# A Strassen pair of third tiles across two halves, in a fused local-attention and ReGLU kernel

## The chip, the cores and the metric

The kernel runs on one core of one Trainium2 chip. The metric is the device time of one execution in microseconds (us). Before the change it is 241.64 us, the median of 3 runs (241.13 to 242.92). Times with two decimals below are from one profiled execution, counted from the start of its span.

## The reference

Attention over 4 batches, 8 heads, 768 positions and head size 64, in which every row sees 8 global keys and a window of 96 local ones, with a bias by distance. Its output, 3072 tokens of 512, goes through a gated feed-forward layer with 1536 hidden columns:

```python
scores = scale * np.matmul(q, k.transpose(0, 1, 3, 2))
keep = is_global | is_local
scores = np.where(keep, scores + bias, -1e9)
a = np.exp(scores - max); a = a / sum(a)
attn_out = np.matmul(a, v)
x = attn_out.transpose(0, 2, 1, 3).reshape(B * S, H * D)
gate = np.maximum(x @ w_gate, 0.0)
val = x @ w_val
return gate * val @ w_out
```

## The kernel before

The work is cut into eight *halves*, numbered c or s from 0 to 7: half a batch each, 384 query positions, three tiles of 128 tokens. For each half there are three kinds of work.

- **Early pieces** (L377): casts of q and k on GpSimd, transposes by DMA, copies that put the keys in order.
- **Attention pieces** (L493), for four pairs of heads p. `QK(p)` is three pieces: `pair_scores` (L386), eight or ten score matmuls into four banks of the `x` PSUM pool (5 banks), with the exps of group 0 on ScalarE (`pair_exps`, L403); then the exps of group 1 and the mask products of group 0 on VectorE (`masks`, L349); then the masks of group 1. `AV(p)` is two pieces, one for each head of the pair (L416): four or five matmuls, a log on ScalarE, and after the second the exp that gives the reciprocal. `N(p)` (L443) is two VectorE products that write the normalized result into `xT`, the input of the feed-forward part.
- **Feed-forward pieces** (`ffn_pieces`, L509). First the weights stage, twelve columns fc of `gate` (four matmuls of 128x384, then a Relu on ScalarE) and `val` (four matmuls, then a VectorE product that writes `ht[:, fc]`). They use the `ff` PSUM pool (3 banks) in turn. Then the output stage: the third tile of the half is multiplied with `w_out` directly (`outp`, twelve matmuls of 128x512), and the first and second tiles together by Strassen's scheme.

The Strassen scheme takes the two tiles as the two rows of a block matrix, the hidden dimension split in two as its columns, and `w_out` as a 2 by 2 block matrix. Seven block products p1 to p7 of six 128x256 matmuls each take the place of eight. Sums and differences of `w_out` blocks (`late["bs"]`) are made once. Sums and differences of `ht` blocks (`cb`, `ad`, `de`) are made for each half on VectorE, some behind the vals of the weights stage (`behind`, L632) and the rest in the output stage (L654). p4, p3 and p1 are copied from PSUM by ScalarE; p2, p5, p6 and p7 are added by VectorE; p6 accumulates into p3's bank and p7 into p1's, and so these banks come free only after the adds of p6 and p7. Results lie in `osb` (3 buffers) and are stored by SyncE's queue, at the very end one of them by ScalarE's.

The order is written by hand: each engine runs its instructions in the order in which the program issues them. `weave` (L664) issues the feed-forward pieces of half c one after the other, counting up their weights (0.65 each, less for the begin), and puts in other pieces by their place, a fraction of the total: the attention of half c+1, spread from 0.0 to 0.8 of half c (for c = 2 from 0.07 to 0.82), and the early pieces of half c+2, from 0.25 to 0.75. So in half 7 no attention is beside the feed-forward work. The first items of a half are `begin` (L546; gate 0 and val 0 on the first three quarters of `xT`) and then the last quarter of gate 0 and of val 0.

In half 6 the issue order around its start and its end is this (other pieces in brackets):

```text
begin [QK0 group 0] g0 [QK0 group 1] v0 g1 [QK0 masks] v1 [QK1 group 0] g2 [QK1 group 1] ...
... g11 [AV2.1] v11 [QK3 masks] o.0 [N2] o.1 [AV3.0] ad o.2 [AV3.1] cb o.3 [N3] p4 de p3 p1 p2 p5 p6 p7
```

Of the kernel before, what the change touches and what calls it, by code (L numbers as in the profile page):

```python
# [8 lines left out]
FP32 = mybir.dt.float32  # L9
BF16 = mybir.dt.bfloat16  # L10
AF = mybir.ActivationFunctionType
ALU = mybir.AluOpType
# [3 lines left out]
def kernel(  # L16
# [12 lines left out]
    nc = tc.nc  # L29
# [4 lines left out]
    DM = H * D  # L34
    DFF = moe_w_gate.shape[1]
    N_DC = DM // 128
    N_FC = DFF // 128
    HP = H // 2
    QH = S // 2
    NN = 3  # L40
# [3 lines left out]
    NHALF = 2 * B  # L44
# [8 lines left out]
    for half in range(2):  # L53
        for j in range(NT):
            w0 = PK * j - 128 * half
            a, b_ = max(0, w0), min(128, w0 + WQ)
# [15 lines left out]
    late = {}  # L72

    PSUM = bass.MemoryType.PSUM
    psum = {}
# [20 lines left out]
    wo_sb = const.tile([128, N_FC, DM], BF16)  # L96
# [264 lines left out]
    def piece_cast(s, p, i):  # L361
        of = (ks_of, qs_of)[i]
        nc.gpsimd.tensor_copy(  # L363
            kqc[:, :, i].rearrange("t n (h d) -> t h n d", d=D)[:, 2 * p : 2 * p + 2],
            of[s][:, 2 * p : 2 * p + 2, :].rearrange("t e (n d) -> t e n d", n=NN))

    def piece_x(s, n):
        nc.sync.dma_start_transpose(
            out=kqT[s % 2].rearrange("d i p t -> d (i p) t")[:, :, n * 128 : (n + 1) * 128],
            in_=kqc[:, n].rearrange("t i z -> t (i z)"))  # L370
# [6 lines left out]
    def early_pieces(s):  # L377
        out = [(0.0, lambda p=p, i=i: piece_cast(s, p, i)) for i in range(2) for p in range(HP)]
        out += [(0.0, lambda n=n: piece_x(s, n)) for n in range(NN)]
        out += [(0.0, lambda p=p: piece_order(s, p)) for p in range(HP)]  # L380
        return out
# [111 lines left out]
    def attention_pieces(s):  # L493
        QK = lambda p: [(0.15, lambda g=g: piece_qk(s, p, g)) for g in range(3)]
        AV = lambda p: [(0.29, lambda e=e: piece_av(s, p, e)) for e in range(2)]
        N = lambda p: [(0.0, lambda: piece_norm(s, p))]
        g = QK(3)
        a = AV(2)
        gap = [(0.0, lambda: None)]
        return (QK(0) + QK(1) + AV(0) + N(0) + gap + QK(2) + AV(1) + N(1) + gap  # L500
                + g[0:1] + a[0:1] + g[1:2] + a[1:2] + g[2:3] + N(2) + AV(3) + N(3))
# [3 lines left out]
    out_v = out.rearrange("(s p n) d -> s n p d", p=128, n=NN)  # L505

    begin_of = {}

    def ffn_pieces(c):  # L509
        ht = ht_pool.tile([128, N_FC, QH], BF16, name="ht")  # L510
        st = {}
# [38 lines left out]
            if c == 2:  # L550
                product(wg, "g", 1, 0, N_DC - 1)


        N2, D2 = N_FC // 2, DM // 2
        tiles_ = [slice(n * 128, (n + 1) * 128) for n in range(2)]

        def sums_of(name, *shape):
            if name not in st:
                st[name] = late["sums"].tile([128, *shape], BF16, name=name)
            return st[name]  # L560

        cb = lambda: sums_of("cb", N2, 2, 128)
        ad = lambda: sums_of("ad", N2, 128)
        de = lambda: sums_of("de", N_FC, 128)

        def sum_cb(i0, i1):
            nc.vector.tensor_tensor(cb()[:, i0:i1].rearrange("f i n t -> f i (n t)"), ht[:, i0:i1, 0:256],
                                    ht[:, N2 + i0 : N2 + i1, 0:256], op=ALU.add)

        def sum_ad(i0, i1):  # L570
            nc.vector.tensor_tensor(ad()[:, i0:i1], ht[:, i0:i1, tiles_[0]],
                                    ht[:, N2 + i0 : N2 + i1, tiles_[1]], op=ALU.add)

        def sum_de(i0, i1):
            x, y = (1, 0) if i0 < N2 else (0, 1)
            nc.vector.tensor_tensor(de()[:, i0:i1], ht[:, i0:i1, tiles_[x]], ht[:, i0:i1, tiles_[y]],
                                    op=ALU.subtract)

        def block(key, pool, left, right, start, stop):
            if start:  # L580
                st[key] = psum[pool].tile([128, 512], FP32, name=f"{pool}_ps")
            for i in range(N2):
                nc.tensor.matmul(st[key][:, 0:D2], lhsT=left(i), rhs=right(i),  # L583
                                 start=start and i == 0, stop=stop and i == N2 - 1,
                                 skip_group_check=not start)
            return st[key][:, 0:D2]

        c0, c1 = slice(0, D2), slice(D2, DM)
        bs = lambda name: lambda i: late["bs"][name][:, i]
        V2 = nc.vector.tensor_tensor  # L590

        def store(n, cols, eng=nc.sync):
            eng.dma_start(out=out_v[c, n][:, cols], in_=st["r", n][:, cols])

        def p4():
            for n in range(2):
                st["r", n] = late["osb"].tile([128, DM], FP32, name="osb")
            ps = block("d", "ff", lambda i: ht[:, N2 + i, tiles_[1]], bs("b21-b11"), True, True)
            nc.scalar.copy(st["r", 0][:, c0], ps)

        def p3():
            ps = block("c", "ff", lambda i: ht[:, i, tiles_[0]], bs("b12-b22"), True, True)
            nc.scalar.copy(st["r", 0][:, c1], ps)

        def p1():
            ps = block("a", "ff", lambda i: ad()[:, i], bs("b11+b22"), True, True)
            nc.scalar.copy(st["r", 1][:, c1], ps)

        def p2():
            ps = block("b", "x", lambda i: cb()[:, i, 1], lambda i: wo_sb[:, i, c0], True, True)  # L610
            V2(st["r", 1][:, c0], ps, st["r", 0][:, c0], op=ALU.add)
            V2(st["r", 1][:, c1], st["r", 1][:, c1], ps, op=ALU.subtract)

        def p5():
            ps = block("e", "x", lambda i: cb()[:, i, 0], lambda i: wo_sb[:, N2 + i, c1], True, True)
            V2(st["r", 0][:, c1], ps, st["r", 0][:, c1], op=ALU.add)
            V2(st["r", 0][:, c0], st["r", 0][:, c0], ps, op=ALU.subtract)
            if c == NHALF - 1:
                store(1, c0)
                store(0, c1)  # L620

        def p6():
            ps = block("c", "ff", lambda i: de()[:, i], bs("b11+b12"), False, True)
            V2(st["r", 1][:, c1], ps, st["r", 1][:, c1], op=ALU.add)
            store(1, slice(0, DM) if c < NHALF - 1 else c1, nc.sync if c < NHALF - 1 else nc.scalar)

        def p7():
            ps = block("a", "ff", lambda i: de()[:, N2 + i], bs("b21+b22"), False, True)
            V2(st["r", 0][:, c0], ps, st["r", 0][:, c0], op=ALU.add)
            store(0, slice(0, DM) if c < NHALF - 1 else c0)  # L630

        behind = {2: [lambda: sum_de(0, 3)], 5: [lambda: sum_de(3, 6)], 8: [lambda: sum_cb(0, 3)],  # L632
                  9: [lambda: sum_ad(0, 3)], 10: [lambda: sum_de(6, 9)]}

        def val_and_sums(fc):
            val(fc)
# [4 lines left out]
        f1 = []  # L641
        for fc in range(N_FC):
            f1.append((0.65, lambda fc=fc: gate(fc)))
            f1.append((0.65, lambda fc=fc: (val if c < 1 else val_and_sums)(fc)))
        f2 = [(0.65, lambda n=n, part=part: outp(n, part))
              for n in (range(NN) if c < 1 else (NN - 1,)) for part in range(4)]
        if c >= 2:
            f1[:2] = [(1.0, begin_of[c][0]), (0.15, begin_of[c][1]), (0.15, begin_of[c][2])]
        if c == 2:
            f1[0] = (1.5, f1[0][1])  # L650
            f1[3] = (0.15, lambda: gate(1, N_DC - 1))
        if c >= 1:
            f2 += [(0.65, f) for f in (p4, p3, p1, p2, p5, p6, p7)]
            for at, f in ((5, lambda: sum_de(9, 12)), (3, lambda: sum_cb(3, 6)), (2, lambda: sum_ad(3, 6))):  # L654
                f2.insert(at, (0.0, f))
        return f1, f2

# [1 line left out]
    def spread(items, first, last):  # L659

        n = len(items)
        return [(first + (i + 0.5) / n * (last - first), f) for i, (_, f) in enumerate(items)]
# [93 lines left out]
    pool = ctx.enter_context(tc.tile_pool(name="late0", bufs=1, side="right", reuse_waits="tile"))  # L756
# [25 lines left out]
    for f in ("m1 g0 m3 v0 m2 g1 K3 K2 m0 g3 K1 S30 S31 g2 K0 S20 v3 S11 v1 S21 A3 N3 v2 S00 S01 "  # L782
              "g5 A2 S10 g4 g6 A0 N2 v5 v4 N0 A1 N1 g7 v7 v6").split():
        i = int(f[1])
# [8 lines left out]
        else:  # L793
# [3 lines left out]
    early.close()  # L797
    ctx.enter_context(open_psum(ff=3, x=5))
    pool = ctx.enter_context(tc.tile_pool(name="late", bufs=1, reuse_waits="tile"))
    late["osb"] = ctx.enter_context(tc.tile_pool(name="osb", bufs=3, reuse_waits="tile"))  # L800
    late["sums"] = ctx.enter_context(tc.tile_pool(name="sums", bufs=1, reuse_waits="tile"))
    late["bs"] = {name: pool.tile([128, N_FC // 2, DM // 2], BF16, name=f"bs{i}")
                  for i, name in enumerate(("b21-b11", "b12-b22", "b11+b22", "b11+b12", "b21+b22"))}

# [14 lines left out]
    for f in (*casts[:7], lambda: nc.gpsimd.tensor_copy(held, wo_sb[0:1, N_FC - 1, 0:1]),  # L819
# [6 lines left out]
    pieces = spread(attention_pieces(2), 0.375, 0.9)  # L826
# [4 lines left out]
          spread([(0.0, lambda name=name, part=part: wo_sum(name, part)) for name in late["bs"] for part in range(2)],  # L831
                 0.1, 0.74))

    for c in range(2, NHALF):
        placed = []
        if c + 1 < NHALF:
            placed.append(spread(attention_pieces(c + 1), *((0.07, 0.82) if c == 2 else (0.0, 0.8))))
        if c + 2 < NHALF:
            load_qk(c + 2, 0, H)
            load_v_half(c + 2)  # L840
            placed.append(spread(early_pieces(c + 2), 0.25, 0.75))
        f1, f2 = ffn_pieces(c)
        weave(f1 + f2, *placed)

# [34 lines left out]
```

## Time and profile before

| | us |
|---|---|
| runs, median of 3 | 241.64 (241.13 to 242.92) |
| the profiled execution | 241.74 |
| its span | 239.9 |
| TensorE (PE) busy | 233.5 |
| VectorE (DVE) busy | 173.3 |
| ScalarE (ACT) busy | 153.4 |
| GpSimd (POOL) busy | 85.9 |
| half 6, first gate to first gate of half 7 | 186.22 to 213.69 |
| half 7, weights stage | 213.69 to 229.28 |
| half 7, output stage on PE | 229.28 to about 236.6 |
| last add on DVE | 236.66 to 237.08 |

A line of the order of time reads: start, duration, engine, line of the kernel, operation, written tile <- read tiles, shapes, count, and in brackets how long the engine had been idle and what released it. PE is the matmul, PEld the weight load that runs beside it. Instructions of a group can overlap, so the start of one to the start of the next (its pitch) can be shorter than its duration. The chain of waits follows the work that ended last back through what released it, with the time of each step.

### The profile page before, as it was taken

To read this page: it belongs to the slowest core of one execution; us is meant where nothing else is said; L and a number is where in the kernel's file an instruction comes from. 1 tells how busy PE (TensorE), PEld (TensorE's weight loads), DVE (VectorE), ACT (ScalarE), POOL (GpSimd) and SP (SyncE) were. 2 spreads that over 40 slices of the span, in tenths; PEclk is the share of its full clock that TensorE was granted. 3 is DMA by queue.
4 is the path that set the end of the run, shared out by engine and by line. 5 is a ranking of instruction groups with operands and counts; after the bars stand their busy time and mean duration, and the time that the engine had idled before them with its cause. 6 is when DMAs were issued, how large, how long until landed. Compare 5 with 4: busy or idle time off the path is not lost.

```text
span 239.9 us, 5355 instructions
## 1 busy us (share of the span) xinstructions
PE 233.5 (97%) x1937; PEld 146.6 (61%) x1945; DVE 173.3 (72%) x456; ACT 153.4 (64%) x347; POOL 85.9 (36%) x202
## 2 busy tenths in 40 slices
PE   7899999999999999999999999999999999999994
PEld 3655555665458566666668566676658566676663
DVE  7775955869677788777787687866887677764643
ACT  5897883337775777748774777638774677733330
POOL 6767893208414860903274060902350000000000
PEclk9999999999999999999999999999999999999999
DMA  6999999993976997098519939398431200030003
GB/s 200 181 198 177 257 234 219 185 162 61 270 178 134 301 150 131 8 185 257 108 25 122 285 93 133 19 166 262 67 68 44 90 0 0 3 129 3 4 27 104
DMA packets 69603, 31.42 MB, mean 131 GB/s; under 512 B 47160, under 2 KB 66616, under 8 KB 69576
## 3 DMA queue, kind: packets, MB, share of 16 engines
q0 software_dynamic: 31744, 8.71, 35.3%
q1 hardware_dynamic: 36616, 21.45, 35.1%
q10 hardware_dynamic: 1216, 0.92, 1.2%
q8 instruction: 15, 0.25, 0.4%
q14 instruction: 12, 0.10, 0.1%
HBM read 28.41 MB, written 6.29 MB: 145 GB/s over the span
## 4 chain that ended last, share of the span: by engine, by line
PE 91%; ACT 3%; DVE 2%; issue 1%; ACTq 0%
PE ff_ps L518 53%; PE ff_ps L538 9%; PE ff_ps L583 8%; PE x_ps L427 6%; PE x_ps L397 4%; PE x_ps L583 3%; PE t_ps L459 2%; PE s_ps L341 2%; PE t_ps L272 1%; PE t_ps L682 1%; ACT lnd L436 1%; PE t_ps L310 1%; DVE xT L446 1%; PE s_ps L321 1%; ACT rcp L441 0%
## 5 line engine op out<-in xcount | busy, mean ns | idle before, releaser
L518 PE MATMUL ff_ps<-xT,wg 128*128 128x384 bf16 x384 | 80.7, 326 | 0.5 <-ACT grelu L525 0.4
L518 PE MATMUL ff_ps<-xT,wv 128*128 128x384 bf16 x384 | 80.2, 326 | 0.0
L531 DVE TENSOR_TENSOR ht<-ff_ps,grelu 128x384 bf16<-128x384 f32 x96 | 53.1, 554 | 28.5 <-PE ff_ps L518 13.8
L525 ACT ACTIVATE grelu<-ff_ps 128x384 bf16<-128x384 f32 x96 | 47.1, 492 | 39.4 <-PE ff_ps L518 20.9
L518 PEld LDWEIGHTS <-wg 128*128 128x128 bf16 x384 | 35.9, 98 | 23.9 <-issue 0.9
L518 PEld LDWEIGHTS <-wv 128*128 128x128 bf16 x384 | 36.1, 97 | 23.4 <-issue 1.2
L406 ACT ACTIVATE es<-x_ps 128x360 bf16<-128x360 f32 (+2 forms) x96 | 36.8, 444 | 16.9 <-PE x_ps L397 16.8
L359 DVE TENSOR_TENSOR es<-es,m_all 128x432 bf16<-128x432 bf16 (+4 forms) x108 | 31.2, 334 | 8.2 <-ACT es L406 7.8
L446 DVE TENSOR_TENSOR xT<-x_ps,rcp 64x384 bf16<-64x384 f32 x48 | 26.6, 554 | 9.4 <-ACT rcp L441 8.8
L436 ACT ACTIVATE lnd<-x_ps 64x384 f32<-64x384 f32 x48 | 23.3, 485 | 12.5 <-PE x_ps L427 11.8
L538 PE MATMUL ff_ps<-wo_sb,ht 128*128 128x512 bf16 x112 | 29.6, 379 | 0.4
L363 POOL CAST kqc<-ks 128x384 bf16<-128x384 f32 x24 | 11.6, 532 | 32.3 <-DMA ks<-in_k_dram 32.3
L137 POOL DMA_DIRECT2D vbuf<-in_v_dram x25 | 21.6, 880 | 2.6 <-DMA wv<-in_moe_w_val_dram 2.1
L427 PE MATMUL x_ps<-es,vbuf 128*128 128x216 bf16 (+4 forms) x216 | 21.8, 225 | 0.0
L427 PEld LDWEIGHTS <-vbuf 128*128 128x128 bf16 x216 | 15.8, 97 | 7.7
L538 PEld LDWEIGHTS <-ht 128*128 128x128 bf16 x120 | 10.8, 97 | 9.8 <-issue 0.2
L263 POOL COPY kT<-kqT 128x240 bf16<-128x240 bf16 x16 | 6.9, 430 | 23.0 <-DMA kqT<-kqc 20.5
L363 POOL CAST kqc<-qs 128x384 bf16<-128x384 f32 x24 | 11.6, 522 | 8.1 <-DMA qs<-in_q_dram 8.1
L259 POOL COPY kT<-kqT 128x360 bf16<-128x360 bf16 x10 | 6.0, 604 | 19.9 <-DMA kqT<-kqc 19.9
L441 ACT ACTIVATE rcp<-lnd 128x384 f32<-128x384 f32 x24 | 12.6, 524 | 0.7
L347 ACT ACTIVATE ef<-s_ps 128x720 bf16<-128x720 f32 (+2 forms) x16 | 10.9, 710 | 2.1 <-PE s_ps L341 1.8
L397 PE MATMUL x_ps<-kqT,kT 64*128 64x216 bf16 (+4 forms) x216 | 11.8, 224 | 0.2
(115 smaller groups left out, 252.8 us busy)
## 6 DMA issues: line engine op xcount, KB each, us to landing
out_dram<-osb SPq DMA_DIRECT2D x22, 256.0 KB, 2.7
ks<-in_k_dram SPq DMA_DIRECT2D x6, 768.0 KB, 5.5
qs<-in_q_dram SPq DMA_DIRECT2D x6, 768.0 KB, 12.1
vbuf<-in_v_dram POOLq DMA_DIRECT2D x21, 120.0 KB, 7.9
wg<-in_moe_w_gate_dram POOLq DMA_DIRECT2D x3, 512.0 KB, 7.9
wv<-in_moe_w_val_dram POOLq DMA_DIRECT2D x3, 512.0 KB, 9.8
wo_sb<-in_moe_w_out_dram POOLq DMA_DIRECT2D x1, 1536.0 KB, 19.6
kq<-in_q_dram ACTq DMA_DIRECT2D x2, 192.0 KB, 4.7
```

Of the source, the lines that this page charges most:

```text
L137: nc.gpsimd.dma_start(out=v_dst(b, NG + r0, NG + r0 + n, j), in_=v[b, :, KT * j + r0 : KT * j + r0 + n, :].rearrange("h p d -> p h d"))
L359: nc.vector.tensor_mul(for_all, for_all, mk)
L363: nc.gpsimd.tensor_copy(kqc[:, :, i].rearrange("t n (h d) -> t h n d", d=D)[:, 2 * p : 2 * p + 2], of[s][:, 2 * p : 2 * p + 2, :].rearrang ...
L406: nc.scalar.activation(es[:, e, 0:c], banks[e][:, 0:c], AF.Exp, bias=0.0, scale=scale)
L427: nc.tensor.matmul(av3[:, :, a : a + w], lhsT=vb[:, j, z0 : z0 + 128], rhs=es[:, e, c : c + NN * w].rearrange("k (n p) -> k n p", n=NN), s ...
L436: nc.scalar.activation(ln[o0 : o0 + 64], av[d0 : d0 + 64, 0:QH], AF.Ln, bias=0.0, scale=1.0)
L446: nc.vector.tensor_tensor(xT_of[s][r, p, :], av_of[s, p, e][r, 0:QH], av_of[s, p, "r"][r], op=ALU.mult)
L518: nc.tensor.matmul(st[key][:, 0:QH], lhsT=w_of(w, dc, fc), rhs=xT_of[c][:, dc, :], start=(dc == 0), stop=(dc == N_DC - 1))
L525: nc.scalar.activation(gr, psg[:, 0:QH], AF.Relu, bias=0.0, scale=1.0)
L531: nc.vector.tensor_tensor(ht[:, fc, :], psv[:, 0:QH], st["gr", fc], op=ALU.mult)
L538: nc.tensor.matmul(ps2, lhsT=ht[:, fc, n * 128 : (n + 1) * 128], rhs=wo_sb[:, fc, :], start=(fc == 0), stop=(fc == N_FC - 1))
L583: nc.tensor.matmul(st[key][:, 0:D2], lhsT=left(i), rhs=right(i), start=start and i == 0, stop=stop and i == N2 - 1, skip_group_check=not s ...
```

## The change

The Strassen scheme is taken out of `ffn_pieces` into a function `strassen(pair, sums, bare)`, in which a pair is any two tiles (half, `ht`, tile number). Halves 1 to 5 use it as before for their first and second tiles, with `outp` for the third. Halves 6 and 7 have no `outp`: their third tiles (half 7's as the first of the pair, half 6's as the second) are a pair of their own, made in half 7's output stage ahead of half 7's own pair, with its own buffers for the sums (`sums3`). Its sums are issued behind vals 1, 6 and 7 of half 7 and at the start of its output stage. `osb` has four buffers.

In half 6 (`bare`) p3 comes before p4, and p4 uses a bank of the `x` pool. The first three attention pieces of half 7, `QK(0)`, are issued in half 5, spread over 0.82 to 0.93 of it; the other 23 are spread over 0.0 to 0.74 of half 6, whose total weight is now 20.15 where it was 22.75.

The issue order that comes of it (a tick marks the pair of third tiles):

```text
half 5:  ... o.3 [N3] p4 de p3 [QK0 group 0] p1 [QK0 group 1] p2 [QK0 masks] p5 p6 p7
half 6:  begin [QK1 group 0] [QK1 group 1] g0 v0 g1 [QK1 masks] v1 [AV0.0] g2 [AV0.1] v2 de [N0] g3 v3 [QK2 ...] ...
         ... g9 [QK3 masks] v9 ad [N2] g10 [AV3.0] v10 de [AV3.1] g11 [N3] v11 ad p3 cb p4 de p1 p2 p5 p6 p7
half 7:  ... v1 cb3(1) ... v6 ad3 ... v7 de3 ... v11
         cb3(0) p4' de3 p3' ad p1' cb p2' de p5' p6' p7' p4 p3 p1 p2 p5 p6 p7
```

The diff, with the parts that only move left out:

```diff
+    def strassen(pair, sums, bare=False):
+        N2, D2 = N_FC // 2, DM // 2
+        st = {}
+        last = pair[0][0] == NHALF - 1 and pair[0][2] == 0
+
+        def h(i, f0, f1):
+            _, ht, n = pair[i]
+            return ht[:, f0:f1, n * 128 : (n + 1) * 128]
...
+        def sum_cb_of(i):
+            V2(cb()[:, :, i], h(i, 0, N2), h(i, N2, N_FC), op=ALU.add)
...
+        def store(i, cols, eng=nc.sync):
+            c, _, n = pair[i]
+            eng.dma_start(out=out_v[c, n][:, cols], in_=st["r", i][:, cols])
...
+        def p4():
+            ps = block("d", "x" if bare else "ff", lambda i: h(1, N2 + i, N2 + i + 1)[:, 0], bs("b21-b11"), True, True)
+            nc.scalar.copy(rows(0)[:, c0], ps)
...
+        return sum_cb, sum_cb_of, sum_ad, sum_de, [(0.65, f) for f in (((p3, p4) if bare else (p4, p3)) + (p1, p2, p5, p6, p7))]
+
+    PAIRED = (6,)
+    third_of = {}
+
     def ffn_pieces(c):
...
+        plain = range(NN) if c < 1 else () if c - c % 2 in PAIRED else (NN - 1,)
+        sum_cb, _, sum_ad, sum_de, products = strassen([(c, ht, 0), (c, ht, 1)], "sums", c in PAIRED)
         behind = {2: [lambda: sum_de(0, 3)], 5: [lambda: sum_de(3, 6)], 8: [lambda: sum_cb(0, 3)],
                   9: [lambda: sum_ad(0, 3)], 10: [lambda: sum_de(6, 9)]}
+        rest = (lambda: sum_ad(3, 6), lambda: sum_cb(3, 6), lambda: sum_de(9, 12))
+        if c in PAIRED:
+            third_of[c] = ht
+        elif c - 1 in PAIRED:
+            _, cb3, ad3, de3, products3 = strassen([(c, ht, NN - 1), (c - 1, third_of[c - 1], NN - 1)], "sums3")
+            behind[1] = [lambda: cb3(1)]
+            behind[6] = [lambda: ad3(0, N_FC // 2)]
+            behind[7] = [lambda: de3(0, N_FC // 2)]
+            rest = (lambda: cb3(0), lambda: de3(N_FC // 2, N_FC)) + rest
...
-              for n in (range(NN) if c < 1 else (NN - 1,)) for part in range(4)]
+              for n in plain for part in range(4)]
...
-            f2 += [(0.65, f) for f in (p4, p3, p1, p2, p5, p6, p7)]
-            for at, f in ((5, lambda: sum_de(9, 12)), (3, lambda: sum_cb(3, 6)), (2, lambda: sum_ad(3, 6))):
+            f2 += (products3 if c - 1 in PAIRED else []) + products
+            places = (2, 3, 5) if plain else (0, 1, 2) if c in PAIRED else (0, 1, 2, 3, 4)
+            for at, f in list(zip(places, rest))[::-1]:
                 f2.insert(at, (0.0, f))
...
-    late["osb"] = ctx.enter_context(tc.tile_pool(name="osb", bufs=3, reuse_waits="tile"))
+    late["osb"] = ctx.enter_context(tc.tile_pool(name="osb", bufs=4, reuse_waits="tile"))
     late["sums"] = ctx.enter_context(tc.tile_pool(name="sums", bufs=1, reuse_waits="tile"))
+    late["sums3"] = ctx.enter_context(tc.tile_pool(name="sums3", bufs=1, reuse_waits="tile"))
...
+    ahead = {}
     for c in range(2, NHALF):
         placed = []
-        if c + 1 < NHALF:
-            placed.append(spread(attention_pieces(c + 1), *((0.07, 0.82) if c == 2 else (0.0, 0.8))))
         if c + 2 < NHALF:
             load_qk(c + 2, 0, H)
             load_v_half(c + 2)
             placed.append(spread(early_pieces(c + 2), 0.25, 0.75))
+        if c + 1 < NHALF:
+            pieces = ahead.pop(c + 1, None) or attention_pieces(c + 1)
+            placed.append(spread(pieces, *(0.07, 0.82) if c == 2 else (0.0, 0.74) if c in PAIRED else (0.0, 0.8)))
+        if c + 1 in PAIRED:
+            ahead[c + 2] = attention_pieces(c + 2)
+            placed.append(spread([ahead[c + 2].pop(0) for _ in range(3)], 0.82, 0.93))
         f1, f2 = ffn_pieces(c)
         weave(f1 + f2, *placed)
```

More of the change, by code (lines that the diff above doesn't have):

```diff
@@ L507, with sums_of, sum_cb, sum_ad @@
     begin_of = {}
+    c0, c1 = slice(0, DM // 2), slice(DM // 2, DM)
+    V2 = nc.vector.tensor_tensor
+    def strassen(pair, sums, bare=False):
[5 more added lines that the diff above has]
+            return ht[:, f0:f1, n * 128 : (n + 1) * 128]
+        def sums_of(name, *shape):
+            if name not in st:
+                st[name] = late[sums].tile([128, *shape], BF16, name=name)
+            return st[name]
+        cb = lambda: sums_of("cb", N2, 2, 128)
+        ad = lambda: sums_of("ad", N2, 128)
+        de = lambda: sums_of("de", N_FC, 128)
+        def sum_cb(i0, i1):
+            ht = pair[0][1]
+            V2(cb()[:, i0:i1].rearrange("f i n t -> f i (n t)"), ht[:, i0:i1, 0:256],
+               ht[:, N2 + i0 : N2 + i1, 0:256], op=ALU.add)
+        def sum_cb_of(i):
+            V2(cb()[:, :, i], h(i, 0, N2), h(i, N2, N_FC), op=ALU.add)
+        def sum_ad(i0, i1):
+            V2(ad()[:, i0:i1], h(0, i0, i1), h(1, N2 + i0, N2 + i1), op=ALU.add)
+        def sum_de(i0, i1):
+            x, y = (1, 0) if i0 < N2 else (0, 1)
+            V2(de()[:, i0:i1], h(x, i0, i1), h(y, i0, i1), op=ALU.subtract)
+        def block(key, pool, left, right, start, stop):
+            if start:
+                st[key] = psum[pool].tile([128, 512], FP32, name=f"{pool}_ps")
+            for i in range(N2):
+                nc.tensor.matmul(st[key][:, 0:D2], lhsT=left(i), rhs=right(i),
+                                 start=start and i == 0, stop=stop and i == N2 - 1,
+                                 skip_group_check=not start)
+            return st[key][:, 0:D2]
+        bs = lambda name: lambda i: late["bs"][name][:, i]
+        def store(i, cols, eng=nc.sync):
+            c, _, n = pair[i]
+            eng.dma_start(out=out_v[c, n][:, cols], in_=st["r", i][:, cols])
+        def rows(i):
+            if ("r", i) not in st:
+                st["r", i] = late["osb"].tile([128, DM], FP32, name="osb")
+            return st["r", i]
+        def p4():
+            ps = block("d", "x" if bare else "ff", lambda i: h(1, N2 + i, N2 + i + 1)[:, 0], bs("b21-b11"), True, True)
+            nc.scalar.copy(rows(0)[:, c0], ps)
+        def p3():
+            ps = block("c", "ff", lambda i: h(0, i, i + 1)[:, 0], bs("b12-b22"), True, True)
+            nc.scalar.copy(rows(0)[:, c1], ps)
+        def p1():
+            ps = block("a", "ff", lambda i: ad()[:, i], bs("b11+b22"), True, True)
+            nc.scalar.copy(rows(1)[:, c1], ps)
+        def p2():
+            ps = block("b", "x", lambda i: cb()[:, i, 1], lambda i: wo_sb[:, i, c0], True, True)
+            V2(st["r", 1][:, c0], ps, st["r", 0][:, c0], op=ALU.add)
+            V2(st["r", 1][:, c1], st["r", 1][:, c1], ps, op=ALU.subtract)
+        def p5():
+            ps = block("e", "x", lambda i: cb()[:, i, 0], lambda i: wo_sb[:, N2 + i, c1], True, True)
+            V2(st["r", 0][:, c1], ps, st["r", 0][:, c1], op=ALU.add)
+            V2(st["r", 0][:, c0], st["r", 0][:, c0], ps, op=ALU.subtract)
+            if last:
+                store(1, c0)
+                store(0, c1)
+        def p6():
+            ps = block("c", "ff", lambda i: de()[:, i], bs("b11+b12"), False, True)
+            V2(st["r", 1][:, c1], ps, st["r", 1][:, c1], op=ALU.add)
+            store(1, c1 if last else slice(0, DM), nc.scalar if last else nc.sync)
+        def p7():
+            ps = block("a", "ff", lambda i: de()[:, N2 + i], bs("b21+b22"), False, True)
+            V2(st["r", 0][:, c0], ps, st["r", 0][:, c0], op=ALU.add)
+            store(0, c0 if last else slice(0, DM))
+        return sum_cb, sum_cb_of, sum_ad, sum_de, [(0.65, f) for f in (((p3, p4) if bare else (p4, p3)) + (p1, p2, p5, p6, p7))]
@@ L551, in begin @@
                 product(wg, "g", 1, 0, N_DC - 1)
[L554 to L630, printed above, removed]
+        plain = range(NN) if c < 1 else () if c - c % 2 in PAIRED else (NN - 1,)
+        sum_cb, _, sum_ad, sum_de, products = strassen([(c, ht, 0), (c, ht, 1)], "sums", c in PAIRED)
         behind = {2: [lambda: sum_de(0, 3)], 5: [lambda: sum_de(3, 6)], 8: [lambda: sum_cb(0, 3)],
```

## The prediction

> **What bounds the kernel now.** I read the page's first part and chain, then busy time by stage, then the order of time around the two joints that the change touches (half 5 to 6, half 6 to 7) and around the last joint inside half 7. All times are us of one profiled execution.
>
> ```profile
> span 239.9 us, 5355 instructions
> PE 233.5 (97%) x1937; PEld 146.6 (61%) x1945; DVE 173.3 (72%) x456; ACT 153.4 (64%) x347; POOL 85.9 (36%) x202
> ...
> PE 91%; ACT 3%; DVE 2%; issue 1%; ACTq 0%
> ```
>
> TensorE is busy 97% of the span and is 91% of the chain that ended last. So an edit pays only if it shortens TensorE's stream, and every wait put into that stream costs its length. By stage (first the stretch, then PE, PEld, DVE, ACT, POOL busy):
>
> ```profile
> 186.20:213.70 27.50, 27.43 (x232) 17.86 (x232) 20.44 (x55) 18.98 (x44) 0.00 (x0) 1.00 0.08 30
> 213.70:237.20 23.50, 22.87 (x151) 14.56 (x149) 12.13 (x28) 7.58 (x16) 0.00 (x0) 1.00 0.13 46
> ```
>
> Half 6 (with the attention of half 7 woven in) is solid TensorE, DVE at 74% and ACT at 69%; half 7 has no attention beside it and both helpers are idle half the time. The granted clock is 1.00 in both. Now the start of half 6, in order of time (start, duration):
>
> ```profile
> 187.29 0.48 PE L397 MATMUL x_ps<-kqT,kT 64*128 64x216 bf16 x10
> 187.64 0.79 ACT L406 ACTIVATE es<-x_ps 128x336 bf16<-128x336 f32 x2 [3.47 <-PE x_ps L397]
> ...
> 188.04 0.81 PE L518 MATMUL ff_ps<-xT,wg 128*128 128x384 bf16 x4
> 188.32 0.50 ACT L525 ACTIVATE grelu<-ff_ps 128x384 bf16<-128x384 f32 x1
> ...
> 188.69 0.85 ACT L406 ACTIVATE es<-x_ps 128x360 bf16<-128x360 f32 x2
> 188.87 0.81 PE L518 MATMUL ff_ps<-xT,wv 128*128 128x384 bf16 x4
> ```
>
> Three ff banks go round: gate 0, val 0, gate 1, then val 1, which takes gate 0's bank. It starts at 188.87, just after the grelu of gate 0 ends (188.82), though gate 1 was through at about 188.69 (188.04 and four at 0.1625). So TensorE already waits 0.18 here, for ACT's queue, in which two exps stand ahead of that grelu.
>
> **The change part by part.**
>
> *Third tiles.* Twelve 128x512 matmuls of a third tile take 2.60 (L538 starts at 229.28, the next block's L583 at 231.88). The seven blocks of a pair are 42 matmuls of 128x256; in the chain of waits 18 of them take 1.97 and 12 take 1.31, 0.109 each, so 4.59. Two third tiles go and one pair comes: 5.20 - 4.59 = 0.61 saved on TensorE. Half 6 becomes 2.60 shorter, half 7 1.99 longer. The added sums are five DVE instructions of 768 columns, 0.56 each by L567; three lie in half 7's weights stage, where a val leaves DVE 0.74 of 1.30 free, two behind its last val.
>
> [...]
>
> *The end of half 7.* After the last val TensorE can run p4' at once, since its left side is half 6's tile. In the trace ht 11 is done 0.84 after TensorE leaves the last val (229.28, L531 ends 230.12). Then DVE runs cb3(0) to about 1.4, de3 to 1.9, ad to 2.2, cb to 2.7; p5' wants cb3(0) at 2.6, p7' wants de3 at 3.9, p1 wants ad at 5.9. All early. p3 takes the bank of p6' at 5.24; DVE reads it until about 5.0 (p2's and p5's four adds at the 0.34 pitch of L611 to L617, one de between). Cost nothing, at most 0.3 if DVE is later. The pair's two 256 KB stores are issued about 2.6 before the next ones, as the third tile's is now (232.69 against 235.21); cost nothing, at most 0.4.
>
> *First scores of half 7, moved into half 5's products.* The ten matmuls of QK(0) cost 0.41 and 0.11 on the matmul behind them, in either place: nothing net. But their five masks now stand in DVE's queue among the adds of the products:
>
> ```profile
> 185.84 0.41 DVE L624 TENSOR_TENSOR osb<-ff_ps,osb 128x256 f32<-128x256 f32 x1
> ...
> 186.54 0.49 PE L518 MATMUL ff_ps<-xT,wv 128*128 128x384 bf16 x2
> ```
>
> Val 0 of half 6 (186.54) takes p3's bank, which p6's add (L624, ends 186.25) releases: 0.29 to spare. Now TensorE comes 0.52 later (187.06). The masks of group 0 fit before p2's adds (exps from 183.42, behind the copy L603, to 184.21; masks 0.65, to 184.9; p2's adds at 185.03). Those of group 1 (two, 0.50 in pitch) stand between p2's and p5's adds: 185.03 + 4 x 0.34 + 0.50 = 186.9 for p6's add, released 187.3. A wait of 0.3; bounds 0 (p5's adds begin early) and 0.6 (group 0's masks too). Behind p6's add wait p7's add and gate 1's bank, with 0.3 to spare.
>
> *Start of half 6.* 23 attention pieces are spread over 0.74 x 20.15 units, 0.648 apart. The first two come at 0.32 and 0.97, both before the 1.0 of begin is through. So QK(1)'s two groups of exps, four and no longer two, are in ACT's queue ahead of gate 0's grelu. The second pair takes 0.70 (188.69 to the next grelu's 189.39). The grelu ends 0.70 later, and val 1's wait grows from 0.18 to 0.88: 0.70 more, between 0.70 and the pair's full 0.85. ACT's rows follow the program's order, so I see no way below.
>
> *End of half 6.* Attention now ends in the weights stage: AV(3) after val 10, the norm after gate 11, then val 11, then p3, p4 with nothing else as cover.
>
> ```profile
> 208.15 0.47 PE L427 MATMUL x_ps<-es,vbuf 128*128 128x216 bf16 x5
> ...
> 208.65 0.48 ACT L436 ACTIVATE lnd<-x_ps 64x384 f32<-64x384 f32 x1 [0.47 <-PE x_ps L427]
> ...
> 209.17 0.53 ACT L441 ACTIVATE rcp<-lnd 128x384 f32<-128x384 f32 x1
> ...
> 209.72 1.12 DVE L446 TENSOR_TENSOR xT<-x_ps,rcp 64x384 bf16<-64x384 f32 x2 [0.59 <-ACT rcp L441]
> ```
>
> From the end of AV's stream (208.46) the norm begins 1.26 later and fills DVE for 1.12. Today the third tile's matmuls cover this; now ht 11 queues behind it and is done at 1.26 + 1.04 (pitch) + 0.56 = 2.9. TensorE in that time has gate 11 and val 11 (1.30), p3 (0.66) and five matmuls of p4 (0.55): 2.5. p4's last matmul needs ht 11, so it waits 0.4. Bounds: 0 (ACT has Ln and Exp sooner) and 0.95 (all of p4 waits). Then ad (ready 3.1, wanted 3.3) and cb (3.6, wanted 4.0) are close but in time.
>
> *In between* the distances from AV to the next scores stay three blocks, so the scores' banks come free as now.
>
> **Sum.** -0.61 + 0.30 + 0.70 + 0.40 = +0.8. The profiled execution took 241.74 (span 239.9 and 1.84 around it), so 242.5; the runs' median is 241.64, 0.1 lower: 242.4.
>
> **The rivals.**
>
> *The waits are hidden (B).* If DVE has released p3's bank in time, ht 11 is 0.4 sooner and something takes ACT's second exps out of the way, only -0.61 is left: 241.0 (240.8 to 241.3). For it: 97% busy TensorE converts a saving one for one. Against: val 1's start at the grelu's end is in the trace.
>
> *DVE falls behind at the end of half 6 (C, slower).* Half 6's DVE work before val 11's end is 14.33 now (186.2 to 206); less QK(0)'s masks 1.25, plus two norms 2.24 and two masks 0.59, it is 15.9 in about 19.4, 82%. Behind val 8 come cb, two masks, ad, a norm, de, a norm and ht 11. My walk leaves the masks 0.5 ahead of AV(3). Each us that DVE is late goes into AV(3) or p4 in full; it decides from about 0.5 late. At 1.2 late: 242.4 + 1.2 = 243.6 (243.2 to 244.6). Against: DVE waits 0.78 for others at 206 now.
>
> *The small blocks do not keep 0.109* because each carries a weight load (0.097 by PEld): they do so today in every half, so I leave this out.
>
> **How the numbers follow.** The forecast 0.55, own range 241.7 (only val 1's wait: -0.61 + 0.70) to 243.8 (-0.61 + 0.6 + 0.85 + 0.95 + 0.4); B 0.25; C 0.15; 0.05 for what I don't see. The range takes B's low end and the forecast's high end, 240.8 to 243.8, and leaves out half of C and the rest. One per cent, about what a measurement of this kernel can tell from no change, is 2.4: under 239.2 no case reaches, 0.02; over 244.1 the upper part of C and a pile of all upper bounds, 0.08; within, 0.90.
>
> **What would show it.** Right: half 7 from its first gate to the end of the last p7 about 24.9 (now 213.69 to 236.6, and 2.0 more); val 1 of half 6 starting at the end of grelu 0, 0.9 after gate 1; p4's last matmul behind ht 11; val 0 of half 6 just behind p6's add. Wrong: those gaps absent (B), or AV(3) of half 7 starting at the end of a mask (C); and a later last landing than 2.7 after the last add.

## The result, and the profile after

| | before | after |
|---|---|---|
| median of 18 runs each, us | 241.70 (240.85 to 242.92) | 242.72 (241.97 to 244.44) |
| ratio to before | | 1.0042 (95%: 1.0027 to 1.0057) |
| profiled span | 239.9 | 241.3 |

The change costs 1.0 us, 0.7 to 1.4 by the interval. That is less than the 1% which the prediction took for the least that can be told from no change, but the interval does not reach down to no change. The side is the one that was forecast (242.4). The page's first part and its chain:

```profile
span 241.3 us, 5408 instructions
PE 233.2 (97%) x1957; PEld 147.8 (61%) x1963; DVE 177.1 (73%) x467; ACT 153.2 (64%) x348; POOL 86.1 (36%) x202
...
PE 84%; DVE 4%; DMA 4%; ACT 4%; issue 2%; POOL 0%; ACTq 0%
```

TensorE's busy time is 0.3 lower and the span 1.4 longer; its share of the chain has gone from 91% to 84%, and DVE and ACT have 4% each, where they had 2% and 3%. (DMA's 4% is one step of 9.41 us on a weight load in the first stage, which the change doesn't touch, so at most three of the seven points belong to the change.) The same two stretches as before, by stage (stretch, then PE, PEld, DVE, ACT, POOL busy):

```profile
186.89:213.03 26.14, 24.86 (x211) 16.45 (x209) 19.54 (x51) 16.87 (x39) 0.00 (x0) 1.00 0.06 21
213.03:238.42 25.39, 24.93 (x182) 17.52 (x179) 16.64 (x39) 8.11 (x18) 0.00 (x0) 1.00 0.14 53
```

Half 6 had 0.07 of TensorE's time not busy; now it has 1.28. The granted clock is 1.00 in both, and a matmul of 384 columns has a mean of 326 ns on both kernels' pages, so it is waiting and no slower matmuls. (The waits counted below are longer in sum. They go from the point where the stream would have had the next matmul, and a matmul's row lasts some 0.16 beyond that point, as with 0.27 for a matmul of 256 columns at a pitch of 0.109; the row still counts as busy.) Four places in the order of time hold it. First the joint of halves 5 and 6:

```profile
185.79 0.60 DVE L359 TENSOR_TENSOR es<-es,m_all 128x384 bf16<-128x384 bf16 x2
...
186.89 0.49 PE L618 MATMUL ff_ps<-xT,wg 128*128 128x384 bf16 x2
186.97 0.42 DVE L595 TENSOR_TENSOR osb<-ff_ps,osb 128x256 f32<-128x256 f32 x1
...
187.43 0.48 PE L618 MATMUL ff_ps<-xT,wv 128*128 128x384 bf16 x2
```

The masks of QK(0) stand in front of p5's adds, p6's add (now L595) ends at 187.39, and val 0 starts at 187.43 instead of 187.21, two matmuls after gate 0. Then val 1:

```profile
188.53 1.52 ACT L406 ACTIVATE es<-x_ps 128x336 bf16<-128x336 f32 x4 [2.96 <-PE x_ps L397]
...
188.92 0.81 PE L618 MATMUL ff_ps<-xT,wg 128*128 128x384 bf16 x4
...
189.91 0.91 ACT L625 ACTIVATE grelu<-ff_ps 128x384 bf16<-128x384 f32 x2
...
190.49 0.81 PE L618 MATMUL ff_ps<-xT,wv 128*128 128x384 bf16 x4 [0.75 <-ACT grelu L625]
```

Four exps stand in a row on ACT where there were two; grelu 0 runs from 189.91 to 190.43, and val 1 starts 0.92 after gate 1's stream is through (188.92 and 0.65), where it was 0.18. The third place was not in the forecast, the scores of QK(2):

```profile
193.90 0.36 DVE L546 TENSOR_TENSOR de<-ht 128x384 bf16<-128x384 bf16 x1
194.18 1.13 DVE L446 TENSOR_TENSOR xT<-x_ps,rcp 64x384 bf16<-64x384 f32 x2
194.44 0.67 PE L397 MATMUL x_ps<-kqT,kT 64*128 64x216 bf16 x10
```

They take 0.67. In the kernel before they took 0.48:

```profile
195.94 0.48 PE L397 MATMUL x_ps<-kqT,kT 64*128 64x216 bf16 x10
```

Their last bank is released by the first of that norm's two products (it ends at 194.72, and the last three score matmuls start from 194.78 on); a de sum now precedes the norm on DVE. And the end of half 6:

```profile
207.85 1.14 DVE L446 TENSOR_TENSOR xT<-x_ps,rcp 64x384 bf16<-64x384 f32 x2
208.45 0.71 PE L552 MATMUL x_ps<-bs,ht 128*128 128x256 bf16 x5
...
209.01 0.56 DVE L631 TENSOR_TENSOR ht<-ff_ps,grelu 128x384 bf16<-128x384 f32 x1
...
209.63 0.28 PE L552 MATMUL x_ps<-bs,ht 128*128 128x256 bf16 x1 [0.47 <-DVE ht L631]
```

ht 11 follows the last norm on DVE, and p4's sixth matmul starts at 209.63 where the stream would have had it at 208.45 + 5 x 0.109 = 209.0: 0.63.

The account: -0.61 for the pair, +0.22, +0.74 (0.92 less 0.18), +0.19 and +0.63: +1.17. Another 0.15 was there before the joint: p4 of half 5 starts at 181.78 and not at 181.63. Together that is 1.32; the two spans, 239.94 and 241.27 with two decimals, differ by 1.33. From the last add to the end of the span it is about 2.85 in both.

### The profile page after: what moved, and what is told of

It is laid out like the page before. It is cut to its first block, busy times and chain, and to the rows that moved or that the text cites. A ratio compares the mean times of both kernels' runs of the same rounds, so it can differ in the third digit from the quotient of the medians.

```text
span 241.3 us, 5408 instructions
## 1 busy us (share of the span) xinstructions
PE 233.2 (97%) x1957; PEld 147.8 (61%) x1963; DVE 177.1 (73%) x467; ACT 153.2 (64%) x348; POOL 86.1 (36%) x202
## 4 chain that ended last, share of the span: by engine, by line
PE 84%; DVE 4%; DMA 4%; ACT 4%; issue 2%; POOL 0%; ACTq 0%
PE ff_ps L618 51%; PE ff_ps L552 9%; PE ff_ps L638 7%; PE x_ps L427 5%; DMA wv<-in_moe_w_val_dram 4%; PE x_ps L397 4%; PE x_ps L552 4%; ACT lnd L436 1%; PE t_ps L715 1%; DVE xT L446 1%; PE t_ps L272 1%; PE t_ps L459 1%; PE s_ps L341 1%; ACT es L406 1%; ACT grelu L625 1%
## 5 line engine op out<-in xcount | busy, mean ns | idle before, releaser
L359 DVE TENSOR_TENSOR es<-es,m_all 128x432 bf16<-128x432 bf16 (+4 forms) x108 | 30.5, 328 | 8.8 <-ACT es L406 8.6
L638 PE MATMUL ff_ps<-wo_sb,ht 128*128 128x512 bf16 x90 | 23.9, 379 | 0.3
L638 PEld LDWEIGHTS <-ht 128*128 128x128 bf16 x96 | 8.6, 97 | 7.6
L546 DVE TENSOR_TENSOR de<-ht 128x384 bf16<-128x384 bf16 (+1 forms) x30 | 11.9, 398 | 0.6
```

Source lines behind the costliest of these rows:

```text
L359: nc.vector.tensor_mul(for_all, for_all, mk)
L638: nc.tensor.matmul(ps2, lhsT=ht[:, fc, n * 128 : (n + 1) * 128], rhs=wo_sb[:, fc, :], start=(fc == 0), stop=(fc == N_FC - 1))
```

## The experiments

The theory: the pair saves its 0.61, and four waits in half 6, each made by one instruction in front of another on a helper's queue, take 1.78 from it. The rivals: the waits have other causes than those instructions; or the pair itself, or the moved attention itself, costs the time. The length of half 6, from its first gate to half 7's first gate, is the measure, as it doesn't hold what happens before. Lengths of other stretches that no edit touches differ by 0.2 and more from kernel to kernel (last section), so the two small waits, 0.19 and 0.22, are read from their rows as well.

**The second exps behind grelu 0**

```diff
-            placed.append(spread(pieces, *... (0.0, 0.74) if c in PAIRED ...))
+            at = spread(pieces, *... (0.0, 0.74) if c in PAIRED ...)
+            if c in PAIRED:
+                at[1] = (0.051, at[1][1])
+            placed.append(at)
```

> The changed kernel with one piece moved in half 6: the second pair of exps of QK(1) is issued after gate 0's grelu, as in the kernel before, and nothing else. Theory (ACT's queue makes val 1 wait): val 1 starts 0.18 after gate 1 is through, not 0.92; half 6 (26.14 long, first gate to first gate) becomes 0.74 shorter, 25.40; the ratio to the kernel before falls from 1.0042 to about 1.001. Rival (TensorE would wait there for another reason, such as the scores' banks or DVE's masks): the wait stays above 0.5 and half 6 stays at 26.1.

Half 6 is 25.42 long, 0.72 less; ratio 1.0020 (1.0003 to 1.0037). The order of time of this kernel:

```profile
188.15 0.81 PE L618 MATMUL ff_ps<-xT,wg 128*128 128x384 bf16 x4
188.44 0.50 ACT L625 ACTIVATE grelu<-ff_ps 128x384 bf16<-128x384 f32 x1
...
188.81 0.85 ACT L406 ACTIVATE es<-x_ps 128x360 bf16<-128x360 f32 x2
188.99 0.48 PE L618 MATMUL ff_ps<-xT,wv 128*128 128x384 bf16 x2
```

The grelu stands between the two pairs of exps again, and val 1 waits 0.19. The two exps in front of that grelu are the whole of the 0.74. One change of place, in ACT's issue order here and in DVE's in the next run, made half 6 0.72 and 0.64 shorter.

**The last norm behind p4**

`at` is the list of places, made as in the experiment above:

```diff
+            if c in PAIRED:
+                at[-1] = (0.81, at[-1][1])
```

> The changed kernel with the last norm of half 7's attention issued in half 6 behind p4 (after the ad and cb sums), no longer ahead of val 11's product; nothing else. Theory (ht 11 stands behind that norm in DVE's queue): ht 11 is done about 0.9 after val 11's stream ends, p4's last matmul no longer waits (0.63 now), half 6 is 0.6 shorter, 25.5; the ratio goes to about 1.0015. Rival (ACT is what is late, its grelu 11 standing behind Ln and Exp): ht 11 comes no more than 0.2 sooner and half 6 stays above 25.9. A third outcome: the norm delays de or p2's adds and the wait reappears at p6 or at val 0 of half 7, half 6 shorter by less than 0.3.

Half 6 is 25.50 long, 0.64 less; ratio 1.0024 (1.0004 to 1.0044). In its order of time ht 11 comes right after its grelu, and p4 is in one piece:

```profile
207.52 0.56 DVE L631 TENSOR_TENSOR ht<-ff_ps,grelu 128x384 bf16<-128x384 f32 x1 [0.21 <-ACT grelu L625]
207.83 0.82 PE L552 MATMUL x_ps<-bs,ht 128*128 128x256 bf16 x6
```

It was DVE's queue and not ACT: ht 11 is done at 208.08, 0.91 after val 11's stream, and p4 wants it at 208.37. A little of the third outcome is there too: val 0 of half 7 starts 0.42 after its gate 0 (211.76 and 212.18) where 0.32 is the stream, as the norm now delays p6's add. That 0.10 falls in half 7 and is not in the 0.64.

**The first de sum one val later**

```diff
+            behind[3] = behind.pop(2)
```

> The changed kernel with half 6's first de sum behind val 3 instead of val 2, so that the first norm of half 7's attention doesn't stand behind it; nothing else. Theory: the scores of QK(2), which take 0.67 in the order of time now against 0.48 for the others, take 0.48 again, half 6 is 0.19 shorter (25.95). Rival (the norm is late because of ACT's reciprocal): no change, 26.14. By time alone this is below what five rounds can tell; the trace decides.

QK(2)'s scores take 0.48 again and half 6 is 25.95 long, 0.19 less:

```profile
194.51 0.48 PE L397 MATMUL x_ps<-kqT,kT 64*128 64x216 bf16 x10
```

The ratio, 1.0045 (1.0027 to 1.0063), can't show so little; the row does.

**The last masks of QK(0) behind p7**

```diff
+            q0 = spread([ahead[c + 2].pop(0) for _ in range(3)], 0.82, 0.93)
+            placed.append(q0[:2] + [(0.999, q0[2][1])])
```

> The changed kernel with the second group of QK(0)'s masks issued after p7 in half 5 instead of between p2 and p5; nothing else. Theory (the masks hold p5's and p6's adds, and so p3's bank): val 0 of half 6 starts right behind gate 0's first two matmuls (0.32 after their start, now 0.54), and half 7's first gate comes 0.22 sooner. Rival (p6's add is late because p2's adds already were): a gain under 0.1. If the masks are now in front of something in half 6, AV(0) of half 7 starts later than now.

Val 0 starts 0.33 after gate 0, half 6 is 25.92 long, 0.22 less, and AV(0) starts 4.02 after the half's first gate (4.24 in the changed kernel), so AV(0) is not late behind the moved masks:

```profile
187.08 0.49 PE L618 MATMUL ff_ps<-xT,wg 128*128 128x384 bf16 x2
187.41 0.49 PE L618 MATMUL ff_ps<-xT,wv 128*128 128x384 bf16 x2
...
191.10 0.47 PE L427 MATMUL x_ps<-es,vbuf 128*128 128x216 bf16 x5
```

Ratio 1.0028 (1.0006 to 1.0050).

**All four moves.** The four edits above in one kernel.

> All four moves together (second exps after grelu 0, last norm behind p4, first de behind val 3, last masks of QK(0) after p7); the pair of third tiles stays. Theory (the pair saves 0.61 and four waits of 0.74, 0.63, 0.19 and 0.22 take 1.78 from it): span about 239.5, ratio 0.9975 (0.996 to 0.999), faster than both kernels by 0.6 and 1.7. Rival (the pair itself, its extra sums or its later stores cost the time): ratio stays at 1.000 or above though the four waits are gone from the trace.

240.88 us (240.42 to 241.91), ratio 0.9966 (0.9942 to 0.9989): faster than the kernel before, and than the changed one. By stage:

```profile
186.45:210.81 24.36, 24.34 (x211) 16.48 (x209) 19.43 (x51) 16.88 (x39) 0.00 (x0) 1.00 0.06 23
210.81:236.29 25.48, 25.02 (x182) 17.51 (x179) 16.87 (x40) 8.13 (x18) 0.00 (x0) 1.00 0.14 52
```

Half 6 has 0.02 not busy, and is 1.78 shorter than in the changed kernel, the sum of the four. Against the kernel before it is 27.47 - 24.36 = 3.11 shorter, the third tile's 2.60 and QK(0)'s 0.5; half 7 is 2.09 longer (1.99 for 14 blocks in place of the third tile and seven, 0.10 for val 0 as above). So the pair itself saves what the sum said, and the rival that it costs is out. The four moves with both third tiles plain were not run; that the gain over the kernel before is the pair's rests on these lengths, and on the run with the moves alone below, in which only 0.22 of the four waits is there to be taken away.

**The pair alone**: half 7's attention stays in half 6, over 0.0 to 0.8.

```diff
-            placed.append(spread(pieces, *... (0.0, 0.74) if c in PAIRED else (0.0, 0.8)))
-        if c + 1 in PAIRED:
+            placed.append(spread(pieces, *... (0.0, 0.8)))
+        if False:
```

> The pair of third tiles and the products' order alone: half 7's attention is issued wholly in half 6, spread from 0.0 to 0.8 as before the change. Theory: half 6's weights are 20.15, so two groups of exps come before gate 0's grelu here too and val 1 waits 0.9; the last norm falls behind p3 and holds the cb sum, p2 waits about 0.6; joint of half 5 and 6 as before. Sum -0.61 + 0.74 + 0.6 = +0.7, ratio 1.003. Rival (the moves of the attention are the cause, not the loss of the third tile's cover): ratio 0.9975.

242.82, ratio 1.0049 (1.0034 to 1.0065). Half 6 is 26.55 long; without the third tile it would be 24.87. Val 1 waits 0.91 here too, and p2 waits 0.90 (0.6 was expected) for a cb sum behind the last norm, which begins at 208.25. Three of p2's matmuls run before the wait, three after it, with p5's six behind them:

```profile
208.25 1.12 DVE L446 TENSOR_TENSOR xT<-x_ps,rcp 64x384 bf16<-64x384 f32 x2
...
208.77 0.49 PE L552 MATMUL x_ps<-wo_sb,cb 128*128 128x256 bf16 x3
...
209.38 0.56 DVE L535 TENSOR_TENSOR cb<-ht 128x768 bf16<-128x768 bf16 x1
...
210.00 1.16 PE L552 MATMUL x_ps<-wo_sb,cb 128*128 128x256 bf16 x9 [0.73 <-DVE cb L535]
```

The two large waits come with the third tile's leaving, not with the moves: its 2.60 had covered the last norm, and its weight is gone from the total by which the attention's places are counted (22.75 to 20.15), which puts a second group of exps before gate 0's grelu.

**The moves alone**: both third tiles plain, the old order of products. The lines left out take away the pair's sums and the order of `bare`.

```diff
-        plain = range(NN) if c < 1 else () if c - c % 2 in PAIRED else (NN - 1,)
+        plain = range(NN) if c < 1 else (NN - 1,)
...
-            f2 += (products3 if c - 1 in PAIRED else []) + products
+            f2 += products
```

> The moves of the attention alone: QK(0) of half 7 in half 5 and the rest over 0.0 to 0.74 of half 6, but the third tiles of halves 6 and 7 plain, twelve 128x512 matmuls each, and the old order of products. Theory: half 6's total is 22.75, the second exps come after grelu 0 and the norm has the third tile as cover; only the joint's 0.22 and perhaps 0.2 at QK(2) are left: +0.2 to +0.4, ratio 1.001 to 1.002. Rival (moving the attention costs by itself): +1.0 or more, ratio 1.004.

241.75, ratio 1.0014 (0.9994 to 1.0034), not told from no change by time. Half 6 is 27.17 long, which is 27.47 less QK(0)'s 0.52 and with the joint's 0.22; no wait at QK(2), at val 1 the old 0.18. By the trace the moves cost 0.22 and no more.

**Both groups of exps behind grelu 0**, on top of the four moves.

```diff
-                at[1] = (0.051, at[1][1])
+                at[0] = (0.051, at[0][1])
+                at[1] = (0.06, at[1][1])
```

> The kernel with all four moves, and in half 6 the scores of QK(1) behind gate 0 and its second exps behind val 0, so that no exp stands ahead of gate 0's grelu. Theory: val 1 starts without the 0.19 that is left of its wait, half 6 is 24.2 long where it was 24.36; ratio 0.996. Rival (the wait moves to gate 2 or val 2, which want ht 0 and grelu 1): half 6 stays at 24.4.

Half 6 is 24.18 long, 0.18 less, and val 1 follows gate 1 at once:

```profile
188.60 0.81 PE L618 MATMUL ff_ps<-xT,wg 128*128 128x384 bf16 x4
189.25 0.81 PE L618 MATMUL ff_ps<-xT,wv 128*128 128x384 bf16 x4
```

Ratio 0.9979 (0.9963 to 0.9996): faster than before, and by time not told from the kernel with four moves.

**Halves 4 and 5 paired too**, on top of the four moves.

```diff
-    PAIRED = (6,)
+    PAIRED = (4, 6)
```

> The kernel with all four moves, and the third tiles of halves 4 and 5 a pair too. Theory (a pair is worth 0.61 wherever its half's joints have no new wait): halves 4 to 7 save 1.22 less 0.1 at each end, ratio 0.994. Rival (half 5 has attention beside its output stage, and DVE, 20.84 of 27.3 busy there now, gets five sums of 0.56 more): new waits in half 5 take the second saving, ratio 0.997 or above.

241.59, ratio 1.0006 (0.9990 to 1.0022): the gain is gone. Half 4 is 24.36 long (27.67 before), as half 6 is with the four moves. Half 5 is 31.11 long; 27.43 in the kernel with four moves and 1.99 for the seven blocks in the third tile's place would be 29.42. Of the 1.7 too much, val 0 at its start waits 0.44 for p6's add, and the scores of half 7's QK(0), in the midst of half 5's products, wait about 1.2:

```profile
182.35 0.24 PE L397 MATMUL x_ps<-kqT,kT 64*128 64x192 bf16 x1 [0.23 <-DVE osb L588]
...
182.55 1.13 DVE L446 TENSOR_TENSOR xT<-x_ps,rcp 64x384 bf16<-64x384 f32 x2
...
183.15 0.31 PE L397 MATMUL x_ps<-kqT,kT 64*128 64x192 bf16 x3 [0.55 <-DVE xT L446]
```

One bank is held by an add of the pair, the next by half 6's last norm, which stands behind the pair's adds on DVE (the two waits come to 1.6). That places the loss at DVE's queue; whether another order would keep the gain was not tried.

## Why the prediction was right

- **The size of the pair**, 0.61: right. Half 7 is 2.00 longer (1.99 forecast), from its first gate to p7's end 24.93 (24.9 forecast), and the kernel with four moves shows half 6's part. Its two terms come from rows of the kernel before: twelve matmuls of 512 columns took 2.60, 217 ns each, and one of 256 columns 109 ns. The small blocks kept that: in the changed kernel's chain 12 of them take 1.31 in half 6 and in half 7.
- **The end of half 7**, cost nothing: right; its 14 blocks run without a gap, and the span ends about 2.85 after the last add, as before.
- **The joint of halves 5 and 6**, 0.30: the mechanism is right, 0.22 measured. p2's adds began at 185.12; the forecast had 185.03, or 185.18 with the 0.15 by which all was later before the joint.
- **The start of half 6**, 0.70: right, 0.74.
- **The end of half 6**, 0.40: right mechanism, a term mis-sized, 0.63. The forecast counted from the end of AV's stream, where the next matmul starts: 208.46 before, 206.50 here. TensorE reached p4's last matmul 2.50 later, at 209.0, as counted ("2.5"). The step that fell short is DVE's side, "1.26 + 1.04 (pitch) + 0.56 = 2.9": ht 11 was done 3.07 later, at 209.57. The norm began after 1.35 and not 1.26; its reciprocal was there at 207.74, but a de sum (207.58 to 207.93) stood in front of it on DVE. ht 11 came 1.16 behind the norm's start and not 1.04; no row shows 1.04, and in the kernel before the instruction behind this norm came 1.14 after its start (209.72 and 210.86). The last 0.06 is from the end of ht 11 to the matmul.
- **"In between the distances from AV to the next scores stay three blocks, so the scores' banks come free as now"**: wrong, by 0.19. The three blocks are right; the step that failed is that it counted distances on TensorE alone and not what else lies between on DVE: the piece N(0) is now behind val 2, which carries a de sum, and was behind val 4, which carries none.
- The sum of +0.8 was low by these last two, +0.42, and 0.04 for the start of half 6, less the joint's 0.08: the trace gives +1.17. The runs' 1.0 (0.7 to 1.4) can't tell the two apart. The range, 240.8 to 243.8, also held rival B and no change at all, so that the time fell in it confirms little; the gaps in the rows, at the places that the prediction named, confirm more.
- **Rival B** (waits hidden, 241.0): not this kernel; the kernel with four moves, in which the waits are gone, takes 240.9. **Rival C** (DVE late before AV(3)): did not happen; the masks end at 204.91 and AV(3) starts right behind gate 10 at 205.24, though with 0.3 in hand and not 0.5.

## What to carry to other kernels

Here, with TensorE 97% busy, a large plain step beside other work was also the cover of that work's last results: without the third tile's 2.60 the last norm, 1.14 of DVE, held p4 for 0.63. Before such a step is taken out, look which result of each helper was finishing under it, and what in that helper's issue order then stands in front of the next instruction that frees a bank. Where work is placed by fractions of a total, taking a step out moves all the rest; print the new issue order and read it queue by queue, with the sums and copies that ride along. Move the instructions that need not be early behind those that free a bank: four such moves, none of them less work, were worth 1.8 us here by the medians (1.7 by the lengths of halves 6 and 7), about three times the saving that they uncovered.

## What the runs showed that was not expected

The eight profiles of kernels with QK(0) in half 5 and halves 0 to 4 as before the change reach half 6's first gate between 185.85 and 187.08, 1.2 us apart, more than the whole effect. The waits in half 6 repeat to some 0.02 us (QK(2)'s was 0.19 in each kernel that had it, val 1's 0.91 or 0.92). Not every stretch repeats so well: half 2, which no edit touches, is 27.86 long in the changed kernel and 28.07 in the one with four moves (27.72 before the change), while half 4 is 27.67 and 27.68 in these two; the runs don't show why. So single spans can't be compared here; the length of a stretch can, but a difference of 0.2 in it counts only when the row of a wait shows it too.
